# Identity and masks of a sparse attention with two MLPs made on GpSimd by index comparisons

## The chip, the cores and the metric

The kernel runs on one core of one Trainium2 chip, in one launch. The core has five engines with a queue each: TensorE (PE in the rows, its weight loads PEld), VectorE (DVE), ScalarE (ACT), GpSimd (POOL) and SyncE (SP). SyncE, ScalarE and GpSimd also issue transfers, and all of these run on the same 16 DMA engines. The metric is the time of one execution in microseconds (us) of device time; the less, the better.

## The reference, cut to what matters

Eight heads of attention over four batches of 576 tokens, head dimension 64. The first four heads see the last 32 positions, the others see the earlier positions of the same residue modulo 32. The 2304 x 512 result goes through two MLPs of width 2048 with different nonlinearities.

```python
rel = pos[:, None] - pos[None, :]
mask_local = (rel >= 0) & (rel < stride)                       # stride = 32
mask_strided = (rel >= 0) & (pos[None, :] % stride == pos[:, None] % stride)
scores = np.where(masks[None], scale * q @ k.T, -1e9)
attn = softmax(scores)                                         # + 1e-09 in the divisor
x = (attn @ v) as (2304, 512)
x = (s * np.maximum(x @ w_in, 0) ** 2 + b) @ w_out             # first MLP; s and b are one number each
h = x @ w_in2                                                  # second MLP
x = np.where(h >= 1, h, np.where(h <= -1, 0, (h + 1) ** 2 / 4)) @ w_out2
```

## The kernel before

**Tiles and stages.** Attention is cut into 21 tiles: 12 strided ones (three for each batch) and 9 local ones of 256 tokens. Tiles 0, 1 and 2 are the strided tiles of batch 0, tiles 3, 4 and 5 local ones, tile 6 the first strided tile of batch 1. Each tile goes through four steps. *Scores* (lines 570 to 599): two matmuls write the mask into two PSUM banks, as identity `idb_t` (128 x 128, bf16) times a mask in `bias_t`; then the products of q and k are added to it. *Softmax* (lines 602 to 629): VectorE takes the maximum, ScalarE the exponential, VectorE or GpSimd scale by the reciprocal of the sum; for tiles 0 to 2 ScalarE does eight exponentials with the sum taken along (line 614, the "shares"). *Flip* (line 637): TensorE transposes the weights against the f32 identity `id_t`. *Values* (lines 653 and 663): weights times v; the result is split into a high and a low part, `xh` (ScalarE, line 328) and `xl` (VectorE, line 695).

The MLPs take `xh` and `xl` in three matmuls for each product (lines 712 to 714, and 955 to 957 in a form with fewer products). Their weights arrive as 64-bit words (`raw`), and ScalarE, VectorE and GpSimd decode them into a high and a low part (`w0h`, `w0l`, `w1h`, `w1l`). The first MLP begins when the first 384 tokens are there, which takes tiles 0 to 4; tile 5 and the later ones lie between its matmuls.

**What the masks are made of.** `masks()` (lines 418 to 430) puts five operations into the plan ahead of all others. ScalarE's queue issues one transfer for `fix_t` (identity, the local mask's rows and the two numbers s and b, `sb_t`) and two for `mask_t` (54 x 54 each, the strided mask). VectorE copies `mask_t` into `bias_t[:, 0]` and the identity into `idb_t` (line 330), ScalarE copies the local mask into `bias_t[:, 1]` in four pieces (line 328). `id_t` and `sb_t` are views of `fix_t`. Ahead of the plan GpSimd fills `mask_t` and `bias_t[:, 2:4]` (lines 1177 to 1180), VectorE fills `warm_t` with zeros, and ten matmuls on `warm_t` keep TensorE busy (line 1185).

**What sets the order.** The program's order is written by a planner (class `Issue`). Each `op(...)` is a step with engines it may run on and an assumed duration; the planner takes next the step that can start first, and among those the one with the earliest due time. To every due time it adds a random number, drawn from a fixed seed in the order in which the steps are listed (line 177). The planner also decides how many matmuls on `warm_t` fill the time before a tile's scores, flip or values (function `busy`, line 568, in the order of the program: they run whether or not TensorE has to wait). Transfers of SyncE's and ScalarE's queues signal their end through eight semaphores that are taken in turn over both queues: a transfer is issued when the one eight places ahead of it has landed.

Of the kernel before, what the change touches and what calls it, by code (L numbers as in the profile page):

```python
# [9 lines left out]
F32 = mybir.dt.float32  # L10
# [5 lines left out]
ALU = mybir.AluOpType  # L16
# [226 lines left out]
def sparse_attention_two_mlps(ctx: ExitStack, tc: tile.TileContext, loc, strd, w_ins, w_outs, fixed, out):  # L243
# [9 lines left out]
    mask_t = sp.tile([128, 1024], F32, name="mask_t", tag="pp", bufs=PP)[:, 0:64]  # L253
    fix_t = const.tile([128, KT + 128 + 2], F32, name="fix_t")
    id_t = fix_t[:, KT:KT + 128]
    sb_t = fix_t[:, KT + 128:]
# [39 lines left out]
    fix_buf, idb_buf, mask_buf, bias_buf = Buf(None, None), Buf(None, None), [Buf(None, None)], [Buf(None, None) for _ in range(2)]  # L296
# [26 lines left out]
    def pe(t):  # L323
        return ("pe", t, 0.1)
# [93 lines left out]
    def masks():  # L418
        op(lambda e: e.dma_start(out=fix_t, in_=fixed[:, 128 + KT:FW]), [("act", 0.5, DMA_LATENCY)], writes=[fix_buf]).sooner = 50.0
        op(lambda e: [e.dma_start(out=mask_t[g * 64:g * 64 + 54, 0:54], in_=fixed[0:54, 0:54]) for g in range(2)],  # L420
           [("act", 1.0, DMA_LATENCY)], part=[mask_buf[0]]).sooner = 49.0
        op(lambda e: copy(e, bias_t[:, 0], mask_t), [("dve", 0.15, 0.1)], [mask_buf[0]], [bias_buf[0]]).sooner = 50.0
        op(lambda e: copy(e, idb_t, id_t), [("dve", 0.2, 0.1)], [fix_buf], [idb_buf]).sooner = 50.0

        def local(e):
            for r in range(4):
                p, c = slice(r * 32, r * 32 + 32), r % 2 * 32
                copy(e, bias_t[p, 1], fix_t[p, c:c + 64])

        op(local, [("act", 0.9, 0.1)], [fix_buf], [bias_buf[1]])  # L430
# [8 lines left out]
    def attend(i, early):  # L439
        kind, b, d = tiles[i]  # L440
        strided = kind == "s"
        if i == 0:
            masks()

# [156 lines left out]
        first = op(scores, [pe(0.95 if strided else 1.1)], [*ins, idb_buf, bias_buf[0 if strided else 1]], sc, allocs=[sm, mx, dn])  # L601
# [37 lines left out]
        turn = op(flip, [pe(0.5)], [sm, fix_buf], [tp], allocs=[pt])  # L639
# [407 lines left out]
    def second_steps(p):  # L1047
        us, affine = (2 * p, 2 * p + 1), []
# [7 lines left out]
        for k, a, b in PRODS:  # L1056
# [13 lines left out]
            if counted and k == 2:  # L1070
                op(lambda e: e.tensor_tensor(out=sums_t[:, 0:KD], in0=sums_t[:, 0:KD], in1=sums_t[:, KD:], op=ADD), [("dve", 0.15, 0.1)],
                   writes=[bias_sum])
                op(lambda e: e.tensor_scalar(out=sums_t[:, 0:KD], in0=sums_t[:, 0:KD], scalar1=sb_t[:, 1:2], scalar2=None, op0=MUL),
                   [("dve", 0.15, 0.1)], [fix_buf], [bias_sum])
                for a_ in affine:
                    a_()
            if ends:
                for c in range(2):
                    j = c + 2 * (r - 1)

                    def last(u=u, j=j):
                        op(lambda e: e.activation(out=x2[u].tile[:, j, :], in_=x2[u].tile[:, j, :], func=AF.Identity,
                                                  scale=sb_t[:, 0:1], bias=sums_t[:, j:j + 1]),
                           [act(n + 200)], [fix_buf, bias_sum], [slot[u][j]], part=touched(u, j))
# [86 lines left out]
    with tc.manual_schedule():  # L1171
# [109 lines left out]
```

## Time and profile before

| what | value |
|---|---|
| time, median of 3 runs (lowest, highest) | 837.6 us (835.99, 840.85) |
| span of the profiled execution | 835.4 us |
| instructions in it | 17740 |
| TensorE matmul busy | 814.1 us, 97% |
| VectorE, ScalarE, GpSimd busy | 75%, 63%, 11% |
| mean granted clock of TensorE | 0.988 |

The page gives the profiled execution by its span alone, from the first instruction to the last; the span lies 2.2 us under the median of the runs. A duration in a row is that of one instruction or of a group ("x16"); what stands in square brackets is the idle time of the engine before it and what ended it. "PEclk" is the share of full speed that TensorE was granted, 0.5 for 1.2 GHz and 1.0 for 2.4 GHz. "SPq" and "ACTq" are transfers being issued by SyncE and ScalarE.

### The profile page before, as it was taken

How to read it: one execution, taken by the hardware profiler on the slowest of the kernel's cores; microseconds unless marked ns; L12 is line 12 of the kernel's file. 1: busy time of each engine (PE TensorE's matmuls, PEld its weight loads, DVE VectorE, ACT ScalarE, POOL GpSimd, SP SyncE). 2: the span in 40 equal slices, each digit the busy share in tenths (PEclk: the TensorE clock that was granted, in tenths of full speed). 3: DMA queues.
4: the chain of work that ended last, by engine and by line, in shares of the span. 5: the costliest groups of instructions: out<-in, count | busy, mean ns of one | idle time of the engine just before them, and what ended most of it. 6: DMA issues, size and time to landing. Idle time of an engine off the chain costs nothing.

```text
span 835.4 us, 17740 instructions
## 1 busy us (share of the span) xinstructions
PE 814.1 (97%) x6296; PEld 791.3 (95%) x6301; DVE 627.6 (75%) x1335; ACT 527.3 (63%) x1120; POOL 93.8 (11%) x186
## 2 busy tenths in 40 slices
PE   6799999989999999999999999999999999999998
PEld 4679999979999999999999999999999999999998
DVE  4598629879666857769779988997477988466966
ACT  5387545655555766757667677965487855667653
POOL 1210002322211114122111010000000000000000
PEclk8799999999999999999999999999999999999999
DMA  8859384798766758889888899988988889888782
GB/s 255 266 192 294 92 275 157 255 302 275 261 238 241 252 202 310 308 292 344 271 305 313 262 395 388 319 248 261 313 255 255 250 251 291 286 254 251 252 264 95
DMA packets 107261, 221.15 MB, mean 265 GB/s; under 512 B 14118, under 2 KB 29606, under 8 KB 107174
## 3 DMA queue, kind: packets, MB, share of 16 engines
q1 hardware_dynamic: 95906, 182.89, 67.9%
q0 software_dynamic: 10240, 36.71, 11.6%
q8 instruction: 50, 0.82, 0.4%
q10 hardware_dynamic: 1028, 0.43, 0.2%
q14 instruction: 37, 0.30, 0.1%
HBM read 172.27 MB, written 47.71 MB: 263 GB/s over the span
## 4 chain that ended last, share of the span: by engine, by line
PE 82%; DMA 6%; issue 6%; DVE 2%; POOL 1%; SPq 1%; ACT 0%; ACTq 0%; POOLq 0%
PE acc L956 7%; PE acc L955 7%; PE acc L957 7%; PE h L712 6%; PE h L713 6%; PE h L714 6%; PE side L956 6%; PE side L955 6%; PE side L957 6%; PE acc L712 3%; PE h L956 3%; PE h L955 3%; PE h L957 3%; PE acc L713 3%; PE acc L714 3%
## 5 line engine op out<-in xcount | busy, mean ns | idle before, releaser
L393 POOL DMA_DIRECT2D dw<-pp x80 | 55.3, 691 | 269.1 <-DVE pp L391 192.2
L712 PE MATMUL h<-xh,w0h 128*128 128x384 f32 x192 | 65.6, 341 | 0.0
L714 PE MATMUL h<-xh,w0l 128*128 128x384 f32 x192 | 64.5, 336 | 0.7 <-DVE w0l L364 0.7
L712 PE MATMUL h<-xh,w0hx 128*128 128x384 f32 x192 | 65.1, 339 | 0.0
L713 PE MATMUL h<-xl,w0h 128*128 128x384 f32 x192 | 64.4, 336 | 0.0
L714 PE MATMUL h<-xh,w0lx 128*128 128x384 f32 x192 | 64.4, 335 | 0.0
L713 PE MATMUL h<-xl,w0hx 128*128 128x384 f32 x192 | 64.4, 335 | 0.0
L739 ACT ACTIVATE t<-h 128x384 f32<-128x384 f32 x51 | 24.9, 488 | 46.6 <-PE h L714 46.3
L714 PEld LDWEIGHTS h<-xh,w0l 128*128 128x128 f32 x192 | 36.0, 188 | 1.0 <-DVE w0l L364 1.0
L712 PEld LDWEIGHTS h<-xh,w0h 128*128 128x128 f32 x192 | 36.1, 188 | 0.5
L713 PEld LDWEIGHTS h<-xl,w0h 128*128 128x128 f32 x192 | 36.1, 188 | 0.3 <-DVE xl L695 0.3
L712 PEld LDWEIGHTS h<-xh,w0hx 128*128 128x128 f32 x192 | 36.0, 188 | 0.3
L713 PEld LDWEIGHTS h<-xl,w0hx 128*128 128x128 f32 x192 | 36.1, 188 | 0.0
L714 PEld LDWEIGHTS h<-xh,w0lx 128*128 128x128 f32 x192 | 36.0, 188 | 0.0
L328 ACT ACTIVATE gh<-w1h 128x384 fp32r<-128x384 f32 x48 | 24.6, 522 | 14.2 <-PE acc L957 6.3
L712 PE MATMUL acc<-gh,w1hx 128*128 128x384 f32 (+1 forms) x96 | 33.4, 348 | 0.0
L712 PE MATMUL acc<-gh,w1h 128*128 128x384 f32 (+1 forms) x96 | 33.2, 346 | 0.0
L1002 DVE TENSOR_TENSOR gl<-w1h,gh 128x384 fp32r<-128x384 f32 x48 | 26.3, 554 | 8.8 <-ACT gh L328 8.5
L751 DVE TENSOR_TENSOR gl<-t,gh 128x384 fp32r<-128x384 f32 x42 | 23.2, 553 | 12.3 <-ACT gh L328 12.3
L714 PE MATMUL acc<-gh,w1lx 128*128 128x384 f32 (+1 forms) x96 | 32.4, 338 | 0.0
L713 PE MATMUL acc<-gl,w1hx 128*128 128x384 f32 (+1 forms) x96 | 32.4, 338 | 0.0
L714 PE MATMUL acc<-gh,w1l 128*128 128x384 f32 (+1 forms) x96 | 32.4, 337 | 0.0
(582 smaller groups left out, 2807.1 us busy)
## 6 DMA issues: line engine op xcount, KB each, us to landing
dw<-pp POOLq DMA_DIRECT2D x60, 512.0 KB, 5.1
w0h<-dw SPq DMA_DIRECT2D x84, 256.0 KB
w0l<-dw SPq DMA_DIRECT2D x84, 256.0 KB
w0hx<-dw SPq DMA_DIRECT2D x84, 256.0 KB
w0lx<-dw SPq DMA_DIRECT2D x84, 256.0 KB
raw<-in_w_ins SPq DMA_DIRECT2D x32, 512.0 KB
raw<-in_w_outs SPq DMA_DIRECT2D x32, 512.0 KB
kb<-dw SPq DMA_DIRECT2D x56, 256.0 KB
```

The lines of the kernel that those rows point to most:

```text
L328: e.activation(out=out, in_=in_, func=AF.Copy)
L393: op(lambda e: e.dma_start(out=dw[o][i][qs].rearrange("q p w n -> p q (w n)"), in_=y.tile[:, 0:nq].bitcast(F32).rearrange("p q w n -> p q ...
L712: e.matmul(out=acc, lhsT=wh, rhs=ah, start=first, stop=False)
L713: e.matmul(out=acc, lhsT=wh, rhs=al, start=False, stop=False)
L714: e.matmul(out=acc, lhsT=wl, rhs=ah, start=False, stop=last)
L739: op(lambda e: e.activation(out=c(t), in_=c(p), func=AF.Relu), [act(n)], [p], [t])
L751: op(lambda e: e.tensor_tensor(out=c(gl), in0=c(t), in1=c(gh).bitcast(F32), op=SUB), [pool(n)] + [dve2(n)], [t, gh], [gl])
L955: e.matmul(out=dst, lhsT=wh, rhs=ah, start=opens and first, stop=False, skip_group_check=not opens)
L956: e.matmul(out=dst, lhsT=wh, rhs=al, start=False, stop=False, skip_group_check=not opens)
L957: e.matmul(out=dst, lhsT=wl, rhs=ah, start=False, stop=last, skip_group_check=not opens)
L1002: op(lambda e, g=g, hi=hi, lo=lo: e.tensor_tensor(out=lo.tile[:, 0:n], in0=g.tile, in1=hi.tile[:, 0:n].bitcast(F32), op=SUB), [dve2(n)], [ ...
```

## The change

`masks()` and its five planned steps are gone, with the tiles `mask_t` and `fix_t`. `id_t` and `sb_t` become tiles of their own. A new function `constants` stands ahead of the plan, where the fills were, and makes everything on GpSimd out of the zeros in `warm_t`: `affine_select` keeps or replaces each element by a comparison of a linear function of its partition and column. There is one for `idb_t`, then four for the strided mask `bias_t[:, 0]`, one for `id_t` and eight for the local mask `bias_t[:, 1]`, 14 in all, and six fills. s and b come by a transfer of 1 KB (`sb_t`) on SyncE's queue, planned where the first MLP's second half begins. The scores and the flip no longer name the constants among what they read.

```diff
-    mask_t = sp.tile([128, 1024], F32, name="mask_t", tag="pp", bufs=PP)[:, 0:64]
-    fix_t = const.tile([128, KT + 128 + 2], F32, name="fix_t")
-    id_t = fix_t[:, KT:KT + 128]
-    sb_t = fix_t[:, KT + 128:]
+    id_t = const.tile([128, 128], F32, name="id_t")
+    sb_t = const.tile([128, 2], F32, name="sb_t")
...
-    def masks():
-        op(lambda e: e.dma_start(out=fix_t, in_=fixed[:, 128 + KT:FW]), [("act", 0.5, DMA_LATENCY)], writes=[fix_buf]).sooner = 50.0
-        op(lambda e: [e.dma_start(out=mask_t[g * 64:g * 64 + 54, 0:54], in_=fixed[0:54, 0:54]) for g in range(2)],
-           [("act", 1.0, DMA_LATENCY)], part=[mask_buf[0]]).sooner = 49.0
-        op(lambda e: copy(e, bias_t[:, 0], mask_t), [("dve", 0.15, 0.1)], [mask_buf[0]], [bias_buf[0]]).sooner = 50.0
-        op(lambda e: copy(e, idb_t, id_t), [("dve", 0.2, 0.1)], [fix_buf], [idb_buf]).sooner = 50.0
...
-        op(local, [("act", 0.9, 0.1)], [fix_buf], [bias_buf[1]])
+    def constants(e):
+        zeros = lambda p, n: warm_t[p, 0:n]
+        every = slice(0, 128)
+        e.affine_select(out=idb_t, in_=zeros(every, 128), pattern=[[-1, 128]], compare_op=ALU.not_equal, fill=1.0, base=0,
+                        channel_multiplier=1)
+        e.memset(bias_t[:, 0], NEG)
+        for g in range(2):
+            p = slice(g * 64, g * 64 + 64)
+            y = bias_t[p, 0, 0:54].rearrange("p (b c) -> p b c", c=NJ)
+            e.affine_select(out=y, in_=zeros(p, 54).rearrange("p (b c) -> p b c", c=NJ), pattern=[[-NJ, 3], [-1, NJ]],
+                            compare_op=ALU.is_ge, fill=NEG, base=0, channel_multiplier=1)
+            e.affine_select(out=y, in_=y, pattern=[[NJ, 3], [0, NJ]], compare_op=ALU.is_ge, fill=NEG, base=NJ - 1,
+                            channel_multiplier=-1)
+        e.affine_select(out=id_t, in_=zeros(every, 128), pattern=[[-1, 128]], compare_op=ALU.not_equal, fill=1.0, base=0,
+                        channel_multiplier=1)
+        for r in range(4):
+            p = slice(r * 32, r * 32 + 32)
+            y = bias_t[p, 1]
+            e.affine_select(out=y, in_=zeros(p, 64), pattern=[[1, 64]], compare_op=ALU.is_ge, fill=NEG, base=-1, channel_multiplier=-1)
+            e.affine_select(out=y, in_=y, pattern=[[-1, 64]], compare_op=ALU.is_ge, fill=NEG, base=STRIDE, channel_multiplier=1)
+        e.memset(bias_t[:, 2:4], 0.0)
+        for r in range(4):
+            e.memset(bias_t[r * 32:r * 32 + 32, 2 + r % 2, 0:32], NEG)
...
-        first = op(scores, [pe(0.95 if strided else 1.1)], [*ins, idb_buf, bias_buf[0 if strided else 1]], sc, allocs=[sm, mx, dn])
+        first = op(scores, [pe(0.95 if strided else 1.1)], ins, sc, allocs=[sm, mx, dn])
...
-        turn = op(flip, [pe(0.5)], [sm, fix_buf], [tp], allocs=[pt])
+        turn = op(flip, [pe(0.5)], [sm], [tp], allocs=[pt])
...
+        if p == 0:
+            op(lambda e: e.dma_start(out=sb_t, in_=fixed[:, FW - 2:FW]), [dma(1024)], writes=[sb_buf])
...
-        nc.gpsimd.memset(mask_t, NEG)
-        nc.gpsimd.memset(bias_t[:, 2:4], 0.0)
-        for r in range(4):
-            nc.gpsimd.memset(bias_t[r * 32:r * 32 + 32, 2 + r % 2, 0:32], NEG)
+        constants(nc.gpsimd)
```

Since five steps leave the head of the planner's list, every later step gets another random number, and the order changes in the whole program. Three places follow; names with numbers are buffers, lines after the change are higher by 5 at lines 576 to 714, and the rows of TensorE, ScalarE and GpSimd stand in the order of their queues.

ScalarE's queue at the start of the program, before: two transfers for the mask, one for `fix_t`, then tile 2's k and q (`k_3`, `q_4`) and v (`w1hx`), with the mask's copies and the copies for tile 2 between them; line 614 is the shares of tile 0.

```order
L420 DMA mask_t<-in_fixed 54x54 x2
L419 DMA fix_t<-in_fixed 128x226
L459 DMA k_3_151<-in_strd 64x2x72 x2
L459 DMA q_4_157<-in_strd 128x2x72
L459 DMA w1hx_159<-in_strd 18x256 x2
L328 ACTIVATE bias_t<-fix_t 32x64 x4
L459 DMA w1hx_159<-in_strd 54x256
L459 DMA w1hx_159<-in_strd 18x256
L328 ACTIVATE k_3_151<-xh_2_137 64x2x18 x2
L459 DMA w1hx_159<-in_strd 18x256 x2
L614 ACTIVATE sm_172,dn_174<-acc_5_170,mx_173 128x64 x4
```

The same place after the change:

```order
L464 DMA k_3_179<-in_strd 64x2x72 x2
L464 DMA q_4_192<-in_strd 128x2x72
L464 DMA w1hx_195<-in_strd 18x256 x2
L464 DMA w1hx_195<-in_strd 54x256
L464 DMA w1hx_195<-in_strd 18x256 x3
L326 ACTIVATE k_3_179<-xh_2_177 64x2x18
L326 ACTIVATE q_4_192<-xh_2_177 128x2x18 x2
L619 ACTIVATE sm_211,dn_213<-acc_6_210,mx_212 128x64 x4
```

The three transfers and the four copies into `bias_t` are gone; the copies ahead of the shares read `xh` (tile 0's inputs) as before.

GpSimd's queue from its first fill to its first step of the softmax (`mx`, line 609), before; `k_3` and `q_4` are the inputs of tile 2, of which a part is copied from the inputs of tiles 0 (`xh_2`) and 1 (`xl_15`); the row `ISA` loads the library of GpSimd's programs.

```order
L1177 MEMSET mask_t 128x64
L1178 MEMSET bias_t 128x128
L1180 MEMSET bias_t 32x32 x4
L330 COPY k_3_151<-xh_2_137 64x2x18 x2
L330 COPY q_4_157<-xh_2_137 128x2x18 x2
L609 ISA
L609 TENSOR_SCALAR mx_173<-mx_173 128x4
```

After, the first of each pair of selects (the rows between repeat them):

```order
L419 ISA
L419 AFFINE_SELECT idb_t<-warm_t 128x128
L421 MEMSET bias_t 128x64
L425 AFFINE_SELECT bias_t<-warm_t 64x54
L427 AFFINE_SELECT bias_t<-bias_t 64x54
...
L429 AFFINE_SELECT id_t<-warm_t 128x128
L434 AFFINE_SELECT bias_t<-warm_t 32x64
L435 AFFINE_SELECT bias_t<-bias_t 32x64
...
L436 MEMSET bias_t 128x128
L438 MEMSET bias_t 32x32 x4
L328 COPY k_3_179<-xh_2_177 64x2x18 x3
L614 TENSOR_SCALAR mx_212<-mx_212 128x4
```

The load of the library stands ahead of all constants, and the copies for tile 2 and `mx` of tile 0 behind them.

TensorE's queue where the first MLP begins, before: the values of tile 4 end (`w1hx_401`), tile 5 is flipped (`sx_544`), weighs its values (`qx`, `qv`), and then the MLP's first matmuls come.

```order
L663 MATMUL side_689<-pt_664,w1hx_401 64x32 x2
...
L637 MATMUL h_732<-fix_t,sx_544 128x128 x4
...
L568 MATMUL side_755<-warm_t 128x256
L663 MATMUL side_754<-pt_733,qx_517 64x32 x2
...
L663 MATMUL side_755<-pt_733,qv_583 64x32 x2
L712 MATMUL h_800<-xh_139,w0h_504 128x384
L713 MATMUL h_800<-xl_140,w0h_504 128x384
```

After:

```order
L642 MATMUL h_723<-id_t,sx_565 128x128 x4
...
L668 MATMUL side_735<-pt_655,w1hx_434 64x32 x2
L581 LDWEIGHTS idb_t
L581 MATMUL side_797<-bias_t,idb_t 128x256
...
L586 MATMUL side_798<-xh_127_717 54x54
L717 MATMUL h_823<-xh_182,w0h_534 128x384
L718 MATMUL h_823<-xl_183,w0h_534 128x384
...
L668 MATMUL side_867<-pt_724,qx_546 64x32 x2
```

The flip of tile 5 has moved ahead of the values of tile 4; between those values and the MLP's first matmul only the scores of tile 6 are left (`xh_127`), and the values of tile 5 come 15 matmuls of the MLP later.

## Rows read from the trace of the kernel before

**Rows 1.** The page: TensorE's busy time, share of the span, instructions.
```profile
PE 814.1 (97%) x6296; PEld 791.3 (95%) x6301; DVE 627.6 (75%) x1335; ACT 527.3 (63%) x1120; POOL 93.8 (11%) x186
```
**Rows 2.** Windows: start:end, length, PE, PEld, DVE, ACT, POOL busy; PEclk, DMA share, GB/s.
```profile
33.33:43.95 10.62, 9.95 (x185) 8.08 (x187) 5.25 (x14) 4.79 (x12) 1.64 (x7) 0.53 0.69 209
43.95:384.00 340.05, 334.65 (x3093) 322.40 (x3086) 249.99 (x574) 207.71 (x440) 66.36 (x125) 1.00 0.74 248
384.00:485.00 101.00, 99.70 (x570) 99.20 (x569) 90.43 (x182) 71.92 (x140) 14.14 (x20) 1.00 0.90 307
485.00:835.40 350.40, 346.86 (x1987) 346.34 (x1985) 264.49 (x511) 226.45 (x454) 4.24 (x7) 1.00 0.83 271
```
**Rows 3.** Chain that ended last, 0 to 46 us: start, us, what.
```profile
13.96 7.39 DMA xl<-in_loc
...
30.43 2.90 issue
...
37.71 1.86 PE side L663 x64
...
42.68 1.34 PE side L663 x64
...
44.74 0.18 PE h L712
```
**Rows 4.** Timeline of the first 22 us: start, us, engine, line, what [idle before <-releaser].
```profile
1.07 0.58 POOL L1180 MEMSET bias_t<- 32x32 bf16 x4
...
1.18 4.45 PE L1185 MATMUL w<-warm_t 128*128 128x512 bf16 x10 [1.18 <-DVE few_t L1175]
...
4.98 0.48 POOL L330 COPY k<-xh 64x36 f32<-64x36 f32 x2 [3.32 <-DMA xh<-in_strd]
...
7.58 0.39 PE L576 MATMUL acc<-bias_t,idb_t 128*128 128x256 bf16 x2 [1.95 <-DVE idb_t L330]
...
9.09 0.25 POOL L609 TENSOR_SCALAR mx<-mx 128x4 f32<-128x4 f32 x1 [3.32 <-DVE mx L603]
...
9.81 0.23 ACT L328 ACTIVATE k<-xh 64x36 f32<-64x36 f32 x1 [1.46 <-DMA xl<-in_strd]
...
10.67 0.31 ACT L614 ACTIVATE sm<-acc,mx 128x64 f32<-128x64 f32 x1 [0.39 <-POOL k L330]
...
20.51 1.05 POOL L628 TENSOR_TENSOR sx<-sx,dn 128x512 f32<-128x512 f32 x1 [5.39 <-DVE dn L627]
...
21.40 0.46 PE L596 MATMUL acc<-xl 64*32 64x64 f32 x32 [1.51 <-DMA xl<-in_loc]
```
**Rows 5.** Windows of the first 33 us, columns as in rows 2.
```profile
8.00:12.00 4.00, 2.17 (x69) 1.74 (x70) 1.85 (x6) 2.12 (x13) 1.68 (x8) 0.64 0.75 211
12.00:31.00 19.00, 15.86 (x392) 11.97 (x394) 14.03 (x43) 12.14 (x58) 3.84 (x6) 0.81 1.02 295
31.00:33.00 2.00, 0.00 (x0) 0.00 (x0) 0.71 (x2) 0.00 (x0) 0.23 (x1) 1.00 0.42 121
```
**Rows 6.** Transfers issued in the first 13 us: out<-in, engine, count, KB each.
```profile
fix_t<-in_fixed ACTq DMA_DIRECT2D x1, 113.0 KB
...
mask_t<-in_fixed ACTq DMA_DIRECT2D x2, 11.4 KB
```
**Rows 7.** Timeline of 39 to 59 us, columns as in rows 4.
```profile
39.47 0.81 POOL L330 COPY k<-xh 64x36 f32<-64x36 f32 x2 [7.37 <-DMA xh<-in_strd]
...
40.12 0.88 DVE L695 TENSOR_TENSOR xl<-side,xh 128x128 fp32r<-128x128 f32 x4 [0.18 <-ACT xh L328]
...
58.69 0.58 ACT L328 ACTIVATE pt<-h 128x512 f32<-128x512 f32 x1
```
**Rows 8.** TensorE's waits from 43 us on: for whom, us in total, times, longest.
```profile
PE side L581 <- DMA kb<-in_strd: 2.7, 2, 1.6
...
PE side L653 <- ACT t L739: 0.6, 1, 0.6
```

More of the change, by code (lines that the diff above doesn't have):

```diff
@@ L295, in sparse_attention_two_mlps @@
     xh, xl, opened = Tokens("xh"), Tokens("xl"), {}
-    fix_buf, idb_buf, mask_buf, bias_buf = Buf(None, None), Buf(None, None), [Buf(None, None)], [Buf(None, None) for _ in range(2)]
+    sb_buf = Buf(None, None)
     serial = [0]
@@ L416, in first_token @@
         return b * S if kind == "s" else t * 256
-    def masks():
-        op(lambda e: e.dma_start(out=fix_t, in_=fixed[:, 128 + KT:FW]), [("act", 0.5, DMA_LATENCY)], writes=[fix_buf]).sooner = 50.0
-        op(lambda e: [e.dma_start(out=mask_t[g * 64:g * 64 + 54, 0:54], in_=fixed[0:54, 0:54]) for g in range(2)],
-           [("act", 1.0, DMA_LATENCY)], part=[mask_buf[0]]).sooner = 49.0
-        op(lambda e: copy(e, bias_t[:, 0], mask_t), [("dve", 0.15, 0.1)], [mask_buf[0]], [bias_buf[0]]).sooner = 50.0
-        op(lambda e: copy(e, idb_t, id_t), [("dve", 0.2, 0.1)], [fix_buf], [idb_buf]).sooner = 50.0
-        def local(e):
-            for r in range(4):
-                p, c = slice(r * 32, r * 32 + 32), r % 2 * 32
-                copy(e, bias_t[p, 1], fix_t[p, c:c + 64])
-        op(local, [("act", 0.9, 0.1)], [fix_buf], [bias_buf[1]])
+    def constants(e):
[21 more added lines that the diff above has]
+            e.memset(bias_t[r * 32:r * 32 + 32, 2 + r % 2, 0:32], NEG)
@@ L441, in attend @@
         strided = kind == "s"
-        if i == 0:
-            masks()
         def room(tag):
@@ L1073, in second_steps @@
                 op(lambda e: e.tensor_scalar(out=sums_t[:, 0:KD], in0=sums_t[:, 0:KD], scalar1=sb_t[:, 1:2], scalar2=None, op0=MUL),
-                   [("dve", 0.15, 0.1)], [fix_buf], [bias_sum])
+                   [("dve", 0.15, 0.1)], [sb_buf], [bias_sum])
                 for a_ in affine:
@@ L1083, in last @@
                                                   scale=sb_t[:, 0:1], bias=sums_t[:, j:j + 1]),
-                           [act(n + 200)], [fix_buf, bias_sum], [slot[u][j]], part=touched(u, j))
+                           [act(n + 200)], [sb_buf, bias_sum], [slot[u][j]], part=touched(u, j))
                     if p == 0 and not k in (2, 4):
@@ L1176, in sparse_attention_two_mlps @@
         nc.vector.tensor_copy(out=ones_t, in_=sums_t[:, 0:4])
-        nc.gpsimd.memset(mask_t, NEG)
-        nc.gpsimd.memset(bias_t[:, 2:4], 0.0)
-        for r in range(4):
-            nc.gpsimd.memset(bias_t[r * 32:r * 32 + 32, 2 + r % 2, 0:32], NEG)
+        constants(nc.gpsimd)
         nc.scalar.activation(out=pre_t, in_=half_t, func=AF.Exp)
```

## The prediction

> **What bounds the kernel now.** I read the page's first part first: TensorE's matmuls fill 97% of the span [rows 1]. A mean hides the stages, so the windows came next. From 43.95 us on TensorE stands still for 340.05 - 334.65 = 5.4 us up to 384, 1.3 us up to 485, and 3.5 us after that, nearly all of it the last outputs on their way out, at a granted clock of 1.00 [rows 2]. The MLPs are thus bound by TensorE's own work, which the change leaves as it is. What is left to win is the first 44 us, where attention waits for data and for itself. There the chain that ended last is the view to read: it runs through a transfer of a local tile's input (issued at 13.96, landed 7.39 us later), a stop of 2.90 us at 30.43 that no event explains, the values of tile 4 (37.71 to 39.57) and those of tile 5, which end at 44.02 with the MLP's first matmul behind them [rows 3]. The DMA engines are 1.02 busy from 12 to 31 us and 0.75 from 8 to 12 [rows 5]. So the front is a burst of loads that saturates the DMA engines, and a chain of small steps at its end.
>
> **Part 1, the three transfers.** They carry 113.0 + 2 x 11.4 = 136 KB [rows 6]. At the 295 GB/s of the saturated stretch [rows 5] that is 0.47 us of all DMA engines. The new transfer of s and b is 1 KB; it sits on SyncE's queue among weight loads, and no row shows a transfer of so many tiny pieces; I bound it between 0 and 0.5 us and take 0, as s and b are not needed for hundreds of us. Since transfers wait for the one eight places ahead, three fewer in ScalarE's queue also let everything behind them go three places sooner; the open quarter of the DMA engines between 8 and 12 us, 4 x 0.25 = 1.0 us, can close. The burst's end thus comes 0.5 to 1.5 us sooner; I take **-1.0 us**. It counts, because TensorE waited 1.51 us for that burst's tile at 21.40 [rows 4], and it stood still from 30.43 to 33.33, while the DMA engines fell to 0.42 busy in 31 to 33 us [rows 5]. The stop came in the middle of a step's matmuls, and ended after the burst did. I read it as tied to the burst, and move it along rather than away.
>
> **Part 2, the constants on GpSimd.** 14 selects and six fills stand in a row. No row shows a select. From below it is bounded by a fill, 0.58 / 4 = 0.145 us, from above by a tensor_tensor of 128x512, 1.05 us; copies and tensor_scalars of a like width take 0.24 and 0.25 us, and a select handles as few elements, so I take 0.25 [rows 4]. The block begins when `warm_t` is zero, as TensorE's first matmul does at 1.18, and takes 14 x 0.25 + 6 x 0.145 = 4.4 us: it ends at 5.6 us (4.1 to 16.7 by the bounds). What the first scores need, five selects and a fill, is there at 1.18 + 5 x 0.25 + 0.145 = 2.6 us. Before, TensorE waited 1.95 us for the identity, from 5.63 to 7.58 [rows 4]; that wait goes, since tile 0's input had landed by 4.98. Scores and maximum took 9.09 - 7.58 = 1.51 us up to `mx` on GpSimd, so `mx` can start at 7.1 instead of 9.09, if the block (5.6) and the three copies ahead of it (0.72) are done: at 6.3 they are, with 0.8 us to spare. ScalarE's shares of tile 0 began at 10.67, after copies that waited 1.46 us for tile 1's input [rows 4]; in the new order only copies of tile 0's input stand ahead of them, so they begin near 7.5, some 3 us sooner. I cost this gain at **0** on the path: it only makes the wait at 21.40 for the burst longer, and the burst is priced in part 1. If the burst did not hold, up to 2.7 us of it would count.
>
> GpSimd's library load now stands ahead of the first select. In the trace it stood ahead of `mx`, in an idle time of 3.32 us which ended with VectorE's maximum [rows 4], so it cost 3.3 us at most; with all of that the block ends at 8.9 us, and `mx` comes 0.8 us later than before, which the wait of 1.51 us at 21.40 takes up. [...]
>
> **Part 3, the order.** The steps' random numbers shift, so the plan is another one. Two places matter. Where the first MLP begins, 44.02 - 39.57 = 4.45 us passed between the values of tile 4 and the MLP: a fill, the flip and the values of tile 5 [rows 3]. In the new order that flip lies earlier, and only the scores of tile 6 stand there, whose input had landed by 39.47; they and the MLP wait for tile 4's low part, done at 40.12 + 0.88 = 41.0 us [rows 7]. Useful work resumes at 41.0 instead of 44.0, 3.0 us sooner; the values of tile 5 come back later, 1.34 us at half speed [rows 3], some 1.1 us as I take it. That leaves 1.9 us. But the clock was 0.53 in that stretch [rows 2]: what is pulled ahead may run at 1.2 GHz, where 2 us do 1 us of work. So -0.9 to -1.9; I take **-1.4 us**. The second place is against it: the flip of tile 8 now stands right before that tile's values, with nothing between them, so TensorE waits for the copy, 0.58 us on ScalarE [rows 7] and the handing over: 0 (if it only replaces the 0.6 us wait that line 653 had [rows 8]) to 1.1 us; I take **+0.5**. The MLP's other waits, five in all from 2.7 down to 0.6 us [rows 8], are drawn anew with the order; I cost that at 0, with 3 us either way in the range.
>
> **Sum.** -1.0 + 0 - 1.4 + 0.5 = -1.9 us. Against the profiled span of 835.4 that is 833.5; the median lay 2.2 us above the span, so 835.7 us.
>
> **The rivals.**
> *The whole front moves.* The burst is not what holds, and the 2.7 us of part 2 count in full, with all of part 3's: 837.6 - 2.7 - 2.6 (1.9 and no wait at tile 8, and the burst's half us hidden in it) gives 832.3 us. For it speaks that `mx` and the shares were late for tile 1's input alone; against it the DMA engines at 1.02.
> *GpSimd is late.* If a select costs 1.05 us, the block ends at 16.7 and `mx` of tile 0 comes at 17.7, 8.6 us late. Waits of 1.51 and 2.90 us take up 4.4, part 3 gives back 0.9: +3.3, so 840.9 us, slower than before. It decides against us once a select costs over 0.8 us (the block then ends at 13.4). Against it: instructions of like size take 0.25.
> *The new order stops the MLPs more often.* Five waits stand there [rows 8], in all 5.4 + 1.3 = 6.7 us [rows 2]; half as much again is 3.4 us, less 1.9: 839.1 us. TensorE has no slack there to hide a late decode.
> *It does nothing.* The stop at 30.43 lasts to 33.33 whatever comes before it, and the pulled-ahead matmuls run at half speed: 837.1 us.
>
> **How the numbers follow.** A difference of 0.5% is 4.2 us, about what a measurement of this kernel can tell from none: faster begins under 833.4, slower over 841.8. Chances: forecast 0.45, whole front 0.17, GpSimd late 0.12, more stops 0.16, nothing 0.10. With the redrawn waits some 15% of the forecast and 85% of the whole front fall under 833.4: 0.07 + 0.14, so faster 0.21. Of late GpSimd and of more stops a half each lie over 841.8, since their prices can grow and not shrink below nothing: 0.06 + 0.08, so slower 0.14, and same 0.65. The range goes from the whole front (832.3, less a little for waits that vanish) to late GpSimd's price: 831.8 to 841.0.
>
> **What would show it.** Right: the first scores at 5.6 to 6 us, `mx` near 7.1, shares from 7.5; selects of 0.25 us and a block that ends by 6.3; the wait for a local tile's input near 21 us longer than 1.51 and over 1 us sooner; the MLP's first matmul at 40 to 42 us. Wrong: an idle time of several us before the first select; a first MLP matmul at 44 us or later; more than 9 us of TensorE waits behind it. If the burst ends no sooner, part 1 falls; if the MLP begins sooner and the time is the same, part 3's gain was lost to waits behind it.

## The result

The changed kernel takes 844.95 us (median of 7 runs, 842.04 to 852.93), the kernel before 838.81 us beside it (7 runs): a ratio of 1.0086, 95% interval 1.0058 to 1.0114. That is 6 us slower, where 1.9 us faster had been forecast, and outside the range. The profiled execution took 844.95 us with a span of 842.9 us, 7.5 us above the span of before.

TensorE's busy time on the page hardly differs from [rows 1]:

```profile
PE 816.7 (97%) x6291; PEld 794.0 (94%) x6291; DVE 623.6 (74%) x1326; ACT 529.9 (63%) x1123; POOL 97.8 (12%) x200
```

The windows answer [rows 2], with the same columns (start:end, length, PE, PEld, DVE, ACT, POOL busy; PEclk, DMA share, GB/s). The first matmul of the MLP comes at 40.52 us, 3.4 us sooner than before:

```profile
40.52:45.50 4.98, 4.98 (x19) 4.66 (x15) 3.41 (x9) 1.37 (x4) 2.64 (x8) 0.50 0.90 336
45.50:64.30 18.80, 18.50 (x330) 16.07 (x329) 16.66 (x41) 14.25 (x34) 3.04 (x4) 1.00 0.61 203
64.30:68.30 4.00, 0.13 (x4) 0.14 (x4) 4.00 (x10) 2.40 (x4) 0.00 (x0) 0.71 0.91 275
68.30:76.30 8.00, 6.35 (x39) 5.78 (x40) 7.56 (x19) 5.60 (x13) 0.53 (x1) 0.50 0.85 294
76.30:151.40 75.10, 75.10 (x803) 71.72 (x802) 38.11 (x92) 36.19 (x80) 9.07 (x23) 1.00 0.50 164
151.40:158.20 6.80, 4.26 (x19) 4.27 (x18) 5.55 (x13) 4.37 (x9) 1.95 (x2) 0.75 0.65 214
158.20:384.00 225.80, 224.58 (x1874) 219.36 (x1873) 165.78 (x375) 140.80 (x290) 50.43 (x95) 1.00 0.76 266
384.00:842.90 458.90, 453.74 (x2596) 452.89 (x2594) 358.46 (x700) 303.29 (x605) 19.66 (x28) 1.00 0.84 278
```

Read PE and PEclk together. The head start is worked at half clock (0.50) until 45.5. From 64.3 TensorE stands still for nearly 4 us, and then works 6.35 us at 0.50. Near 151 the same happens on a smaller scale (a wait of 2.5 us, then 3.5 us at 0.51). Before, the clock was 1.00 in all of that [rows 2], and the stretch in which tile 8's values stood (at 64.47, without a wait) was full:

```profile
64.00:76.00 12.00, 11.99 (x89) 11.37 (x88) 9.60 (x23) 8.59 (x21) 0.00 (x0) 1.00 1.01 307
```

TensorE's waits of the changed kernel behind 40.6 us, beside [rows 8] (for whom, us in total, times, longest):

```profile
PE side L658 <- ACT w0hx L326: 3.9, 1, 3.9
PE h L642 <- DVE sm L633: 2.5, 1, 2.5
PE side L960 <- DMA kb<-dw: 1.6, 1, 1.6
PE side L586 <- DMA kb<-in_strd: 1.2, 1, 1.2
PE h L718 <- DVE xl L700: 0.9, 1, 0.9
PE h L717 <- ACT xh L326: 0.7, 1, 0.7
```

The longest is the wait of tile 8's values. Its surroundings in the timeline (start, us, engine, line, what [idle before <-releaser]):

```profile
62.53 0.45 PE L601 MATMUL side<-xh 64*32 64x64 f32 x32
62.80 0.59 PE L601 MATMUL side<-xl 64*32 64x64 f32 x32
...
63.70 0.63 PE L642 MATMUL h<-id_t,sx 128*128 128x128 f32 x4 [0.30 <-ACT w1h L326]
...
64.36 0.60 ACT L326 ACTIVATE pt<-h 128x512 f32<-128x512 f32 x1 [0.75 <-PE h L642]
...
66.13 0.42 DVE L608 TENSOR_REDUCE mx<-side 128x4 f32<-128x256 f32 x1
...
67.67 0.75 DVE L625 TENSOR_TENSOR sm<-side,mx 128x256 f32<-128x256 f32 x2
...
68.19 1.19 PE L658 MATMUL side<-pt,qv 36*64 36x36 f32 x24 [3.87 <-ACT w0hx L326]
```

Line 601 is the scores of tile 9. They now stand *ahead* of tile 8's flip (63.70) and values (68.19); in the kernel before they came behind both, with some 145 MLP matmuls between. Tile 8's copy `pt` was done at 64.96, so it was not late. But the scores of a tile and the values of a tile share two PSUM banks (`side`), and tile 9's scores hold both until VectorE has subtracted the maximum from them (line 625, at 67.67, the first of two ending near 68.1). VectorE came to that late, since weight decodes stand between its steps. The row names ScalarE's `w0hx` as the releaser, which had nothing to do with the values but ended last before them: this was the reading to be tested.

### The profile page after: what moved, and what is told of

Read it like the earlier page. It is cut to its first block, busy times and chain, and to the rows that moved or that the text cites. A ratio compares the mean times of both kernels' runs of the same rounds, so it can differ in the third digit from the quotient of the medians.

```text
span 842.9 us, 17752 instructions
## 1 busy us (share of the span) xinstructions
PE 816.7 (97%) x6291; PEld 794.0 (94%) x6291; DVE 623.6 (74%) x1326; ACT 529.9 (63%) x1123; POOL 97.8 (12%) x200
## 4 chain that ended last, share of the span: by engine, by line
PE 88%; DMA 7%; DVE 2%; ACT 1%; issue 1%; SPq 0%; ACTq 0%; DVEq 0%
PE acc L961 8%; PE acc L962 8%; PE acc L960 8%; PE h L717 8%; PE h L718 8%; PE h L719 8%; PE side L960 6%; PE side L962 6%; PE side L961 6%; PE acc L717 4%; PE acc L718 4%; PE acc L719 4%; PE h L961 3%; PE h L960 3%; PE h L962 3%; DMA raw<-in_w_ins 2%
## 5 line engine op out<-in xcount | busy, mean ns | idle before, releaser
L718 PE MATMUL acc<-gl,w1h 128*128 128x384 f32 (+1 forms) x96 | 33.2, 345 | 0.0
L346 ACT ACTIVATE dt<-raw 128x512 f32<-128x512 f32 x42 | 27.6, 669 | 8.1 <-DMA raw<-in_w_ins 3.6
```

The costliest lines, as they stand in the source:

```text
L346: first = op(lambda e: e.activation(out=x(), in_=words(1).bitcast(F32), func=AF.Prelu, scale=2.0 ** -112, alpha=-2.0 ** 32), [act(DM)], [r ...
L718: e.matmul(out=acc, lhsT=wh, rhs=al, start=False, stop=False)
```

## An account of the span

For every kernel below the profiled span is, to within 1.5 us in all but one, the start of the first MLP, plus TensorE's idle time behind it (gaps over 0.15 us), plus half of the time worked at half clock behind it, plus the idle matmuls that an experiment put in, plus 785 us. These 785 us are the work at full clock and the last outputs; they are taken from the rows themselves (before: 835.4 - 43.95 - 6.69 = 784.8), so the table divides the span up and does not forecast it. "Idle behind" and "work at half clock" are counted behind the MLP's start, in us, in one profiled execution of each kernel:

| kernel | MLP begins | idle behind | work at half clock | sum | span |
|---|---|---|---|---|---|
| before | 43.95 | 6.69 | 0 | 835.6 | 835.4 |
| changed | 40.52 | 11.14 | 14.79 | 844.1 | 842.9 |
| e1_old_order | 42.16 | 6.70 | 0 | 833.9 | 834.0 |
| e2_new_order_loaded | 43.16 | 11.29 | 13.27 | 846.1 | 845.2 |
| e3_scores9_later | 41.02 | 11.92 | 8.42 | 842.2 | 841.9 |
| e4_fill_wait (3.4 filled) | 38.66 | 8.08 | 9.81 | 840.1 | 839.6 |
| e5_tile8_first | 39.28 | 8.79 | 9.25 | 837.7 | 838.3 |
| e6, the same filled (2.4) | 40.05 | 11.29 | 7.61 | 842.5 | 843.0 |
| e7_one_stop | 42.46 | 14.48 | 6.71 | 845.3 | 846.2 |
| e8_stop_filled (5.3 filled) | 41.87 | 10.00 | 6.83 | 845.6 | 844.8 |
| b_seed4 | 40.23 | 11.34 | 8.98 | 841.1 | 841.2 |
| a_seed4 | 40.94 | 12.45 | 19.53 | 848.2 | 847.6 |
| a_seed5 | 42.13 | 8.84 | 3.41 | 837.7 | 838.4 |
| a_seed6 | 42.09 | 14.33 | 0 | 841.4 | 845.8 |

Between before and changed: -3.4 us of start, +4.45 us of idle time, +7.4 us of half clock, together +8.4 of the 7.5 measured. By this account the clock costs more than the waits. In the row of e8 the half clock holds 3.4 us of the idle matmuls themselves; without them the sum would be 843.9. Of a_seed6 some 4 us remain unexplained: 3.2 of them lie in the 4079 MLP matmuls of 128x384, which took 720.9 us without their waits, against 717.7 in the kernel before, at a granted clock of 1.00 in both; why, no run shows.

The starts in the second column are single readings. The kernels changed, e3, e4, e5 and e6 have the same instructions up to there, and begin the MLP between 38.66 and 41.02 us; e1, e7 and e8, which differ there by one fill, between 41.87 and 42.46. A difference of 1 or 2 us between two single traces is therefore not yet a difference between two kernels.

## The experiments

Each ratio is against the kernel before on the same chip.

**Order or constants.** e1 keeps the new constants, and leaves five empty steps in the planner's list, so that every other instruction stands where it stood before:

```diff
+    def masks():
+        none = lambda e: None
+        op(none, [("act", 0.5, DMA_LATENCY)], writes=[fix_buf]).sooner = 50.0
+        op(none, [("act", 1.0, DMA_LATENCY)], part=[mask_buf[0]]).sooner = 49.0
...
         constants(nc.gpsimd)
```

> The constants are made on GpSimd as in the changed kernel and the three transfers are gone, but five empty steps stand in the planner's list where the mask's steps were, so that the order of all other instructions is the one of the kernel before; the 1 KB of s and b is loaded beside the first half's results of the first MLP. Theory (the loss comes from the new order alone: tile 9's scores take the two PSUM banks that tile 8's values need, and after the wait TensorE runs at half clock): 835 to 838.5 us, no idle time over 2 us on TensorE between 50 and 160 us, and a granted clock of 1.00 there. Rival (the constants themselves, or the free places in the transfer queue, cost it): 843 us or more.

Measured: 838.19 us, ratio 0.9999 (0.9978 to 1.0020). In its trace the first MLP begins 1.8 us sooner than before, and the stop "issue" of [rows 3] is still there, at the same place (the 959th of TensorE's instructions in both traces):

```profile
32.89 0.24 PE L679 MATMUL side<-pt,w1lx 64*64 64x32 f32 x1 [2.75 <-issue]
...
42.16 0.44 PE L728 MATMUL h<-xh,w0h 128*128 128x384 f32 x1
```

Of the 1.8 us, 0.4 were there when the stop ended (32.89 against 33.33). The rest came behind it, in a stretch with 8.78 us of work instead of 9.95 and a clock of 0.63 instead of 0.53 (window of e1, beside the first of [rows 2]):

```profile
32.89:42.16 9.27, 8.78 (x185) 6.94 (x187) 5.15 (x14) 4.79 (x12) 0.79 (x4) 0.63 0.80 244
```

e2 is the counterpart: the changed order, with the transfers and copies back ahead of the plan.

```diff
-        constants(nc.gpsimd)
+        for g in range(2):
+            nc.scalar.dma_start(out=mask_t[g * 64:g * 64 + 54, 0:54], in_=fixed[0:54, 0:54])
+        nc.scalar.dma_start(out=fix_t, in_=fixed[:, 128 + KT:FW - 2])
+        nc.vector.tensor_copy(out=bias_t[:, 0], in_=mask_t)
...
```

> The counterpart: the order of the changed kernel to the last instruction, but masks and identity come by ScalarE's three transfers, issued ahead of all planned work, and VectorE copies them; no select on GpSimd. Theory (order): 844 to 848 us, with a wait of about 3.9 us before tile 8's values near 65 us and a granted clock of 0.5 behind it, as in the changed kernel. Rival (the constants on GpSimd cost it): 836 to 840 us.

Measured: 844.23 us, ratio 1.0075 (1.0050 to 1.0101), with the same wait to the hundredth:

```profile
70.57 1.19 PE L636 MATMUL side<-pt,qv 36*64 36x36 f32 x24 [3.87 <-ACT w0hx L328]
```

So the order makes the loss; a part of the constants in it can't be told from none (1.0075 against 1.0086, with overlapping intervals).

**Who holds tile 8's values.** e3 moves tile 9's early steps behind the last step of tile 8:

```diff
-        for o in self.order():
+        done = self.order()
+        mine, next_ = ([o for o in done if starts[i].n <= o.n < ends[i]] for i in (8, 9))
+        at = done.index(mine[-1])
+        late = [o for o in done[:at] if o in next_]
+        done = [o for o in done[:at] if o not in late] + [mine[-1]] + late + done[at + 1:]
+        for o in done:
```

> The changed kernel with one part of its order moved: all steps of tile 9 that stand ahead of tile 8's last step (its scores on TensorE above all) follow behind that last step. Theory (tile 9's scores hold the PSUM banks): the wait of 3.87 us before tile 8's values is under 1.2 us, the clock stays at 1.00 behind it, and the time is 845 - 3.9 - 5.1 + up to 3 for tile 9's later steps: 836 to 840 us. Rival (something else holds the values, or the slow stretch has a cause of its own): a wait over 3 us stays in front of the values and the time is 843 us or more.

Measured: 843.25 us, ratio 1.0072 (1.0051 to 1.0093). The wait went as forecast, the time did not: 843 us or more was the rival's number.

```profile
64.83 0.68 PE L664 MATMUL side<-pt,qv 36*64 36x36 f32 x24 [0.69 <-ACT pt L331]
...
70.54 0.83 DVE L706 TENSOR_TENSOR xl<-side,xh 128x72 fp32r<-128x72 f32 x4
...
70.99 0.83 PE L587 MATMUL side<-bias_t,idb_t 128*128 128x256 bf16 x2 [5.49 <-DVE xl L706]
```

The values now wait only for their copy, 0.69 instead of 3.87 us: tile 9's scores did hold them. But the scores behind them wait 5.49 us for the same two banks, which tile 8 holds until VectorE's `xl`, which again stands behind decodes. The wait was not removed but turned round. My sum had left out that the two tiles exclude each other either way, and that the MLP's next tokens need tile 8's result anyway.

e5 therefore moves both: on every engine tile 8's values and their splitting stand directly behind the copy `pt`, ahead of the decodes, and tile 9's early steps come 40 MLP steps later.

```diff
+        tail = mine[-5:]
+        done = [o for o in done if o not in tail]
+        at = done.index(mine[-6]) + 1
+        done[at:at] = tail
+        at = done.index([o for o in done[at + 5:] if o.eng == "pe" and o not in next_][40])
+        late = [o for o in done[:at] if o in next_]
+        done = [o for o in done[:at] if o not in late] + late + done[at:]
```

> The changed kernel with two moves in its order: tile 8's values and the splitting of their result stand on every engine directly behind the copy that they read (ahead of the decodes that were before them), and tile 9's scores with the steps that follow on them come 40 of TensorE's MLP steps (120 matmuls) later. Theory (tile 9's early scores and the decodes ahead of tile 8's evacuation made TensorE wait, once for banks and once for the first MLP's second group, which reads tile 8's result): no wait over 1.5 us between 50 and 150 us, clock 1.00 from 50 to 150 us, 845 - 3.9 - 0.7 - 0.9 - 5.1 = 834.4, with up to 3 us of new waits 834 to 838 us. Rival (the stretch is limited by the weights' arrival, whatever the order): waits of together over 3 us come back elsewhere ahead of 80 us, and 841 us or more.

Measured: 841.03 us, ratio 1.0039 (1.0021 to 1.0057), 4 us better than the changed kernel, 3 us short of the forecast, and just at the rival's 841 us. No wait near tile 8 is over 1.39 us, but four of them add up to 3.0 us and the clock still falls. None of the four ends with a transfer, as the rival had it. The longest ends when VectorE's last step on tile 8's weights (`sx`, until 61.57) and ScalarE's decode `w1h` (until 61.64) are done, the others with tile 8's copy, `xh` and `xl`:

```profile
60.33:69.97 9.64, 6.61 (x42) 5.83 (x43) 7.26 (x17) 4.29 (x10) 0.00 (x0) 0.65 0.75 241
```

**The clock.** e4 leaves the changed order and puts 15 idle matmuls of 128x512 between tile 8's flip and values:

```diff
+            for _ in range(15 if i == 8 else 0):
+                e.matmul(out=tp.tile.rearrange("p a b -> p (a b)"), lhsT=warm_t[:, 0:128], rhs=warm_t, start=True, stop=True)
```

> The changed kernel with 15 idle matmuls of 128x512 on zeros between tile 8's flip and its values, so that TensorE works through most of the wait; the wait itself stays, up to 0.5 us more of it. Theory (the 10 us at half clock behind the wait follow from TensorE's standing still in it, and are 5 us of the loss): granted clock 1.00 from 66 to 76 us, and 839.5 to 841.5 us. Rival (the clock falls for another cause, or half clock costs little): clock 0.5 there all the same, or 844 to 846 us.

Measured: 842.54 us, ratio 1.0059 (1.0031 to 1.0086). TensorE works through the wait but for 0.69 us ahead of the idle matmuls, and the half-clock stretch shrinks from 10.2 us to the 3.4 us behind two later waits of 1.05 and 1.20 us (first the window of the filled wait, then that one):

```profile
61.55:68.96 7.41, 4.43 (x40) 2.13 (x39) 7.17 (x18) 4.85 (x12) 0.53 (x1) 1.00 0.96 322
68.96:72.38 3.42, 3.41 (x11) 3.41 (x12) 3.37 (x8) 2.30 (x6) 0.00 (x0) 0.50 0.75 222
```

The time lies 1 us above the forecast range. The direction is the forecast one; the gain is some 2 us instead of 5, and as the two intervals overlap it is not clear of noise.

e6 fills the waits of e5 in the same way, with 6 matmuls of 128x512 ahead of the flip and 8 of 128x216 ahead of the values.

> The order with tile 8 first, and idle matmuls in tile 8's two waits (6 of 128x512 ahead of the flip, 8 of 128x216 ahead of the values), 2 us of them. The order alone gave 841.0 us, with 6.8 us at half clock from 63.1 us on, behind waits of 1.39, 0.69 and 0.64 us. Theory (a wait costs its length and then half of the time that TensorE works at half clock): the stretch from 63 to 70 us is at clock 1.00, the waits stay as long as before when the idle matmuls are counted as waiting, and 841 - 3.0 = 838 us (837 to 839), level with the kernel before. Rival (the clock follows something else, or the idle matmuls cost what they save): 840.5 us or more.

Measured: 841.11 us, ratio 1.0052 (1.0030 to 1.0075): no gain, and over the 840.5 us of the rival that the idle matmuls cost what they save. In its place the filling did what it should, 7.68 us at full clock for the steps that took e5 9.86 us (60.33 to 70.19):

```profile
61.42:69.10 7.68, 6.42 (x57) 4.93 (x58) 5.85 (x15) 3.46 (x9) 0.00 (x0) 1.00 0.77 237
```

But at 75.44 its TensorE waits 1.46 us for ScalarE's `t`, which e5's does not: a part of what the clock gave back was lost to the next wait. Its profiled execution also waits 6.3 us behind 160 us, e5's 3.3, above all for transfers (`kb`, 2.2 and 2.1 us, against 1.8 and 0.9); that execution took 844.82 us, 3.7 over the median, so these waits need not be in the others. What took the gain in the median is open.

e7 and e8 price one stop by itself, in e1's kernel, in the midst of the first MLP. ScalarE copies from PSUM, GpSimd fills the tile 18 times, and TensorE's next matmul reads it; e8 adds 66 idle matmuls (the loop of 66 in the code below is e8's alone).

```diff
+                e.matmul(out=p.tile[:, 0:128], lhsT=pause_t, rhs=pause_t, start=True, stop=True)
+                nc.scalar.activation(out=pause_t, in_=p.tile[:, 0:128], func=AF.Copy)
+                for _ in range(STOPS):
+                    nc.gpsimd.memset(pause_t, 0.0)
+                for _ in range(66):
+                    e.matmul(out=p.tile[:, 128:256], lhsT=idb_t, rhs=idb_t, start=True, stop=True)
+                e.matmul(out=p.tile[:, 0:128], lhsT=pause_t, rhs=pause_t, start=True, stop=True)
```

> The price of one stop by itself: the kernel with the old order and the constants on GpSimd (838.2 us), in which TensorE is made to stand still once in the first MLP's matmuls near 70 us, where neither it nor GpSimd had a wait: ScalarE copies 128x128 values from PSUM and GpSimd then fills the same tile 18 times (some 0.2 us each, near 4 us in all) before TensorE's next matmul may read it. Everything else is unchanged. Theory: the stop's length L plus half of the time worked at half clock behind it, as in the changed kernel (there 6.4 us, so 3.2 us): 838.2 + 4 + 3.2 = 845.4 us (844 to 847), with a granted clock of 0.5 for some us behind the stop. Rival (a stop costs its own length, the clock's fall belongs to the early part of the program): 842 us and clock 1.00.

> The same stop, with 66 idle matmuls of 128x128 on TensorE while it lasts (3.5 us at 2.4 GHz by the 0.053 us that 128 of 2400 columns per us take); the MLP's next matmul comes no sooner than without them. Theory (the second half of the price is the clock, and the clock follows TensorE's standing still): clock 1.00 behind the stop and 838.2 + 4 = 842.2 us (841 to 843.5), some 3 us less than with the stop unfilled. Rival (the clock follows the stop of real work, or the extra comes from something else, such as work on other engines that piles up): the same time as unfilled, 844 us or more.

Measured: 848.02 us (ratio 1.0121, 1.0091 to 1.0150) and 845.80 us (1.0101, 1.0067 to 1.0135). Both lie above their forecasts (844 to 847, 841 to 843.5), and e8 above the 844 us of its rival. The stop was longer than meant, 7.13 us, as the copy stood behind a decode that waited for a transfer, and 18 fills took 4.84 us. The idle matmuls waited for that copy too, so they fill 5.3 of e8's 7.4 us, 3.4 of these at half clock (0.51 from 71.68 to 75.09). Of e7 the stop in the timeline, and the window behind it; of e8 the idle matmuls, and the window behind them:

```profile
76.08 0.29 PE L759 MATMUL h<-pause_t 128*128 128x128 bf16 x1 [7.13 <-POOL pause_t L758]
```

```profile
76.08:79.38 3.30, 3.30 (x11) 3.30 (x12) 0.00 (x0) 0.00 (x0) 0.00 (x0) 0.50 0.02 5
```

```profile
70.40 5.47 PE L760 MATMUL h<-idb_t 128*128 128x128 bf16 x66 [2.06 <-ACT pause_t L756]
```

```profile
75.71:79.00 3.29, 3.29 (x23) 3.29 (x21) 0.38 (x1) 0.84 (x2) 0.00 (x0) 1.00 0.00 1
```

The same 12 MLP matmuls took 3.67 us behind the empty stop (76.13 to 79.80) and 2.16 us behind the filled one (75.74 to 77.90). So in these two traces the half clock behind the stop goes with TensorE's standing still in it, and costs 1.5 us. The medians differ by 2.2 us, but their intervals overlap, as those of e4 and the changed kernel do, and e6 shows no gain: that the clock falls behind a stop is shown in place, what it is worth in the time of the whole kernel is not shown beyond the noise.

**Other draws of the order.** Only the seed of the planner's random numbers is changed (3 to 4, 5, 6), in the changed kernel (a) and in the one before (b).

> The changed kernel with another seed (4 for 3) for the random numbers added to the due times: the same constants, another order throughout. Theory (the changed kernel drew a bad order by chance; an order is worth several us either way): anything from 833 to 847 us, within 3 us of what its waits on TensorE behind 41 us and its stretches at half clock add up to, and not the pattern of tile 9's scores ahead of tile 8's flip with a wait of 3 us or more. Rival (without the mask's steps the planner starts tile 9 early whatever the draw): 843 us or more, with that pattern.

> The changed kernel with seed 5. Expectations as for seed 4: by the theory 833 to 847 us, and differing from seed 3 and seed 4 by more than the 2 us of a measurement's uncertainty; by the rival 843 us or more.

> The changed kernel with seed 6, a fourth draw of its order. Theory (the draw decides): between 833 and 850 us, with its waits on TensorE and the half-clock work behind the first MLP's start accounting for it within 1 us: span = start of the MLP + idle time behind it + half of the time worked at half clock behind it + 785 us, as for the other kernels. If it lies under 835 us, a draw is enough to beat both kernels.

> The kernel before (masks and identity loaded) with seed 4 for 3. Theory (the draw decides, not the constants): it differs from 838 us by up to 8 us, and seed 3 happened to be a good draw (the kernel's seed had been there when the rest was tuned), so slower is likelier than faster: 837 to 846 us. Rival (orders are worth no more than 1 or 2 us, and the changed kernel's loss is special): 836 to 840 us.

| order drawn with | masks loaded | made on GpSimd |
|---|---|---|
| list of before, seed 3 | 1 | 0.9999 (e1) |
| list of before, seed 4 | 1.0068 (b_seed4) | 1.0079 (e9) |
| changed list, seed 3 | 1.0075 (e2) | 1.0086 (the change) |
| changed list, seed 4 | 1.0178 | 1.0132 (a_seed4) |
| changed list, seed 5 | 1.0011 | 1.0015 (a_seed5) |
| changed list, seed 6 | | 1.0106 (a_seed6) |

Each has an interval of 0.002 to 0.004 either way. Down a column, the draw is worth up to 1.8%, and none of the five other orders beats the one the kernel had; one, the changed list with seed 5, can't be told from it. Three of the six show the pattern of tile 9 ahead of tile 8. In b_seed4, with its masks loaded, it is the changed kernel's wait over again; in a_seed4 it is nearly so:

```profile
61.83 0.59 PE L596 MATMUL side<-xl 64*32 64x64 f32 x32
...
62.72 0.63 PE L637 MATMUL h<-fix_t,sx 128*128 128x128 f32 x4 [0.30 <-ACT w1h L328]
...
67.22 1.19 PE L653 MATMUL side<-pt,qv 36*64 36x36 f32 x24 [3.87 <-ACT w0hx L328]
```

```profile
64.31 0.59 PE L601 MATMUL side<-xl 64*32 64x64 f32 x32
64.85 0.65 PE L642 MATMUL h<-id_t,sx 128*128 128x128 f32 x4
68.97 0.43 PE L658 MATMUL side<-pt,qv 36*64 36x36 f32 x4 [3.46 <-ACT dt L346]
```

That falsifies a part of what I expected of a_seed4: the pattern is not seed 3's own, and its 848.77 us lie above the 847 us that I allowed. a_seed5 (838.47 us) shows that the changed list does not bring it every time. a_seed6 (846.24 us) lies in its range, but the account misses its profiled span by 4.4 us where 1 us was expected.

**Does the front's gain arrive?** Three more pairs of equal order, with and without the transfers:

> A second pair for the constants alone: the instruction order of the kernel before with seed 4 (844.5 us with loaded masks), constants made on GpSimd, the three transfers gone. Theory A (the constants and the free queue places are worth the 1.8 us by which the first MLP began sooner with seed 3): 842.7 us, ratio to the kernel before 1.0047. Theory B (what the front gains is given back in waits for transfers behind it): 844.5 us, ratio 1.0068.

> A third pair: the order of the changed kernel with seed 4 (848.8 us with constants on GpSimd), masks and identity loaded by ScalarE's three transfers. Theory A: 2 us more, 850.6 us, ratio 1.0154. Theory B: the same, 848.8 us, ratio 1.0132.

> A fourth pair: the order of the changed kernel with seed 5 (838.5 us with constants on GpSimd), masks and identity loaded. Theory A: 840.3 us, ratio 1.0037. Theory B: 838.5 us, ratio 1.0015.

Measured: 843.79 us (ratio 1.0079), 852.44 us (1.0178) and 838.78 us (1.0011). Across the rows of the table, constants on GpSimd cost 0.0, +0.1, +0.1, -0.5 and +0.0%. Four pairs of five show no gain; one does, by 3.9 us, with the widest interval, which overlaps its partner's. Their mean, -0.04%, is 0.4 us. In e1 the front's 1.8 us are in the profiled span only (834.0 against 835.4), and that execution took 835.77 us, 2.4 under the median. Of the five pairs' traces four begin the MLP 1.4 to 2.6 us sooner with the constants on GpSimd, one (seed 5) 1.6 us later; why the medians do not follow is open.

## Why the prediction was wrong, point by point

**Right: GpSimd's part of the front.** Most of what was to show it came out so. The selects take 0.29 us at 128x128 and 0.23 to 0.24 us at the smaller shapes (0.25 was taken), the block ends at 6.31, the first scores start at 5.00 (5.6 to 6 was forecast), `mx` at 7.10, and the wait for tile 1's input takes up what was gained, as [rows 4] suggested:

```profile
1.20 0.29 POOL L419 TENSOR_SCALAR_AFFINE_SELECT idb_t<-warm_t 128x128 bf16<-128x128 bf16 x1 [0.77 <-DVE few_t L1182]
...
2.89 0.29 POOL L429 TENSOR_SCALAR_AFFINE_SELECT id_t<-warm_t 128x128 f32<-128x128 bf16 x1
...
5.00 0.38 PE L581 MATMUL acc<-bias_t,idb_t 128*128 128x256 bf16 x2
...
5.72 0.59 POOL L438 MEMSET bias_t<- 32x32 bf16 x4
...
7.10 0.25 POOL L614 TENSOR_SCALAR mx<-mx 128x4 f32<-128x4 f32 x1
...
8.14 0.30 ACT L619 ACTIVATE sm<-acc,mx 128x64 f32<-128x64 f32 x1
...
9.72 0.62 PE L586 MATMUL acc<-xl 64*54 64x54 f32 x32 [3.14 <-DMA xl<-in_strd]
...
20.95 0.46 PE L601 MATMUL acc<-xl 64*32 64x64 f32 x32 [1.68 <-DMA xl<-in_loc]
```

The first select begins 0.02 us behind the first matmul. The several us of idle time that were named as a sign of being wrong are not there: GpSimd is idle for 0.77 us in all ahead of the first select, the library load included (two `MODIFY_POOL_CONFIG` of 0.011 us each, at 0.8). The shares came at 8.14 rather than 7.5, behind a copy on ScalarE that waited for a transfer until 7.64.

**Part 1, -1.0 us: not borne out.** The open quarter of the DMA engines between 8 and 12 us did not close; the share there was 0.75 before [rows 5] and is less now:

```profile
8.00:12.00 4.00, 1.98 (x61) 1.62 (x61) 1.50 (x6) 3.24 (x23) 1.34 (x7) 0.92 0.66 215
```

Tile 1's input came at 9.72, no sooner than before (9.50 for the matmul that reads it), and the local tile's near 21 us at 20.95 instead of 21.40: 0.45 us sooner, where over 1 us was named as the sign. e1 begins the MLP 1.8 us sooner, more than forecast, but mostly by what lies behind the stop at 33 us, and four pairs of five show nothing of it in the median.

**Part 3, the first place, -1.4 us: the clock was priced too low.** 3.0 us were taken for the work pulled ahead. Against e1, which has the same constants, the MLP begins 1.6 us sooner, and the last to come ahead of it was not tile 4's low part, as the prediction had it (`xl`, waited for until 37.48), but the transfer of tile 6's input:

```profile
39.59 1.00 PE L586 MATMUL side<-xh 64*54 64x54 f32 x32 [1.43 <-DMA xh<-in_strd]
```

That the MLP began near the forecast 41 us is thus in part luck. And 4.98 us behind its start are worked at half clock, 2.5 us of loss, which e1 and before do not have. The prediction knew of the half clock there and let it take back at most 1.0 us.

**Part 3, the second place, +0.5 us: this is the step that failed.** The place was right, tile 8's flip directly ahead of its values. Its price was put at 0 to 1.1 us, for the copy of the weights alone. Three things were left out: that the scores of tile 9 had come between, that scores and values share two banks, which puts VectorE's queue of decodes into the wait, and that the clock fell behind the wait. It measured 3.87 us, with 0.71 and 0.94 us of waits for tile 8's result behind it, and half of 6.35 us: 8.7 us in the profiled execution, against a term of 0.5. How much of that is lost in the median no run isolates; e5, which removes the long wait but not the fall of the clock, is 4 us faster than the changed kernel.

**Part 3, the rest, 0 with 3 us either way: wrong in its middle.** The wait at 151 us costs 2.5 us and half of the 3.4 us of half clock behind it; the other waits fell from 6.7 us (seven waits, where the prediction counted the five rows of [rows 8]) to 3.1. But 0 was no fair middle: with the constants on GpSimd, the five other draws lie 0.15 to 1.3% above the drawn order of before, 0.8% or 7 us on average. If that order was kept because it was good, which no run shows, a new draw could only be expected to be worse.

**The rivals.** "The new order stops the MLPs more often" is what happened; its price of 839.1 us lacked the clock. Half as much waiting again was assumed, and 11.1 us against 6.7 is 1.7 times; these 11.1 us are over the 9 us that the prediction named as a sign of being wrong. The half clock's 7.4 us weigh more than that. "GpSimd is late" is refuted by the selects' times. "It does nothing" is wrong for the change as a whole; for the constants alone, e1 and three other pairs come out so in the median, though its reason fails: the stop that it held fixed at 33.33 ended at 32.89 in e1 and is missing in the changed kernel.

## What to carry to other kernels

Where a step is added to or taken from a planner that breaks ties at random, compare kernels of equal order first (empty steps in the list do it) and judge the new order as a draw of its own. Look for the clock that a wait on a busy TensorE costs behind it (in the changed kernel 0.50 from 68.30 to 76.30, behind the wait of 3.87 us). And look for which steps share a buffer with the one that waits: the releaser that the trace names may only be the last to end (`w0hx` here), and moving one of two that exclude each other just turned the wait round in e3 (0.69 us ahead of the values, 5.49 ahead of the scores).

## What the runs showed of the hardware

Behind 7.13 us of standing still of a full TensorE the granted clock was 0.50 for 3.3 us of work (e7); behind the same stop with 5.3 us of it filled with idle matmuls it was 1.00 (e8). In e5 no single wait near tile 8 was over 1.39 us, and the clock fell all the same, to 0.65 over 60.33 to 69.97, where four that add up to 3.0 us came close together. An `affine_select` on GpSimd took 0.23 to 0.29 us for up to 128 columns in the changed kernel. Idle matmuls of 128x256 in the kernel before stood 0.109 us apart at 16.19 us, where PEclk was 1.00, and 0.213 us apart at 36.22, where it was 0.50: 2350 and 1200 columns per us, which is what the 2.4 and 1.2 GHz ahead of the prediction and in it, and the 2400 columns of e8, stand for.

The unexplained stop of 2.90 us that ended at 33.33 [rows 3] does not go with the order. In e4, whose instructions are those of the changed kernel up to there, it takes 1.12 us, and in the changed kernel itself it is missing:

```profile
32.59 0.25 PE L670 MATMUL side<-pt,w1lx 64*64 64x32 f32 x3 [1.12 <-issue]
```

Eleven of the seventeen traces have it, with 0.28 (a_seed4) to 3.33 us (e7), in each of them at the 958th or 959th of TensorE's instructions, in old and new orders. In each of them it ends 1.3 to 1.6 us behind the end of a transfer of 16 KB on the queue q8, whose kind the DMA view names "instruction" (before: 30.88 to 31.90; e1: 30.35 to 31.45). In the window of 30 to 33 us of the kernel before that is this row:

```profile
q8 instruction: 1, 0.02, 2.1%
```

In the other six traces TensorE comes to that place about when such a stop would have ended, or later, and does not stop. What TensorE waits for there was not shown; that it is its next instructions, behind a burst of loads, is the author's guess from the name of that kind and from these times.
